# Retention and a feed-forward layer on one core: other orders of the same work in steps 0 to 31

## The chip, the core and the metric

The kernel runs on one core of one Trainium2 chip. Its engines work side by side, each through a queue of its own: TensorE (PE, matrix products), VectorE (DVE), ScalarE (ACT), GpSimd (POOL), and SyncE (SP), which here issues all transfers. The metric is the device time of one execution, in microseconds (us).

## What is computed

Eight batches of eight heads with 576 positions of 64 numbers go through a retention layer (scores with a decay by distance, no softmax); its result x, 4608 rows of 512, goes through a feed-forward layer whose activation is a quotient of two polynomials.

```python
scores = scale * np.matmul(q, k.transpose(0, 1, 3, 2))
Dmat = np.where(rel >= 0, gamma[:, None, None] ** rel[None, :, :], 0.0)
attn = np.matmul(scores * Dmat[None, :, :, :], v)
x = attn.transpose(0, 2, 1, 3).reshape(B * S, H * D)          # 4608 x 512
h = x @ w_in                                                  # 512 -> 2048
P = a[0] + a[1] * h + a[2] * h2 + a[3] * h3                   # h2 = h*h, h3 = h2*h
Q = 1.0 + np.abs(b[0]) * np.abs(h) + np.abs(b[1]) * h2
out = (P / (Q + 1e-06)) @ w_out                               # 2048 -> 512
```

## The kernel before

**Tiles.** The 4608 rows are 36 units of 128 rows; four units make a block of 512 rows (nine blocks). w_in and w_out are cut into 16 slices each. Every float32 operand of a big product is split into a high and a low part that TensorE takes in its fast float32 form, and three of the four products of parts are summed: xhi and xlo for x, w[:, 0] and w[:, 1] for a weight slice, g[:, 0] and g[:, 1] for the activation.

**Steps.** A step i handles one pair (block b, slice f). Steps 0 to 7 are block 0 with slices 0 to 7, steps 8 to 23 block 1 with all 16, steps 24 to 31 block 0 with slices 8 to 15; from step 32 on a block has 16 steps in a row. In the names of tiles the two numbers are block and slice (h0_7, p1_3), and a weight slice is w0_f (w_in) or w1_f (w_out).

**What a step consists of**, by function (lines 390 to 490):
- `gemm1` (12 matmuls) makes h of this step in one of two PSUM buffers `h`.
- `ffn_p`: ScalarE writes p and u = |h|, VectorE multiplies p by h. `ffn_p2`: VectorE, the last operation that reads h and so frees its buffer.
- `ffn_va` (ScalarE) and `ffn_v` (VectorE) make v, the denominator.
- One step later: `ffn_r` (ScalarE: Ln and Exp into u, the reciprocal), `ffn_q` and `ffn_q3` (VectorE: three operations on p, v and u).
- Two steps later: `ffn_hi` (ScalarE) and `ffn_lo` (GpSimd up to step 25, VectorE later) split p into the parts of g.
- `gemm2` (12 matmuls) three or four steps later adds g times w_out into two accumulators `acc`. When a block's last slice is done, ScalarE copies the accumulators to `o`; for block 0 this happens after slice 7 (step 11), and block 1 uses the same two buffers from step 12 on.

**Attention.** A *visit* (lines 297 to 311) finishes unit a and begins unit k on TensorE: at steps 0, 2, 4, 6, 23, 24, 26, 28, 30, then every fourth. The begun part lies in `y`, which takes one of the two `h` buffers, and in `ps`. Before it, `scale_q` (GpSimd, qk) and `scale_v` (ScalarE, eight small operations on kv) prepare unit k; after it, `decay`, `decay1` and `add` (VectorE) read y and ps, `fade` (GpSimd) scales the state S, and `keep_hi` (ScalarE) and `keep_lo` (VectorE) write xhi and xlo of unit a.

**Splitting weights.** During steps 0 to 23 the weights, loaded as raw bits, are split by `split_weight`: ScalarE makes two arrays (`start`), VectorE combines them in two operations on c (stages `split1` and `split2`), then ScalarE writes the high part w and GpSimd the low part w (`split3`). `split_step(j)` advances every split that has reached stage j, so a name that stands ahead of an earlier stage's name takes effect a step later.

**What sets the order.** Each engine runs its instructions in program order (class `InOrder`). Within a step the program order comes from a list of names, walked by `run`: `FIRST` in steps 0 to 7 and 21 to 23, `MID` in steps 8 to 20 (where u lies in PSUM, as `free_at`), `DENSE` in steps 24 to 31, `REST` later. A name whose work doesn't occur in a step is passed over.

Of the kernel before, what the change touches and what calls it, by code (L numbers as in the profile page):

```python
# [29 lines left out]
NF = DFF // P  # L30
# [1 line left out]

BEFORE = "split1 start scale_q scale_v visit_a decay visit_b add fade keep_hi keep_lo split2 split3 split0".split()
LAST_BEFORE = "visit_b keep_hi visit_a keep_lo start split1 decay add fade scale_q scale_v split2 split3 split0".split()
FIRST = (
    "split1 gemm1 visit ffn_p split2 ffn_p2 ffn_hi decay keep_hi ffn_lo gemm2 ffn_r scale_q split3 decay1 add fade keep_lo"
    " start scale_v split0 ffn_q ffn_q3 ffn_va ffn_v"
).split()
MID = (
    "split1 split2 gemm1 ffn_p ffn_r ffn_hi ffn_lo split3 ffn_va gemm2 ffn_p2 ffn_q ffn_v ffn_q3 start split0"  # L40
).split()
DENSE = (
    "gemm1 split1 ffn_p visit ffn_p2 decay keep_hi decay1 add fade keep_lo split2 split0 ffn_va ffn_v scale_q ffn_hi ffn_r"
    " ffn_lo scale_v gemm2 split3 ffn_q ffn_q3"
).split()
REST = (
    "gemm1 ffn_p visit ffn_p2 ffn_hi decay keep_hi ffn_lo decay1 add fade keep_lo scale_q scale_v ffn_va ffn_v gemm2 ffn_r"
    " ffn_q ffn_q3"
# [1 line left out]
END = "ffn_r ffn_hi gemm2 ffn_lo ffn_q ffn_q3".split()  # L50
# [5 lines left out]
VISITS = {0: (4, 5), 2: (5, 6), 4: (6, 7), 6: (7, None), 23: (None, 8)}  # L56
# [20 lines left out]
def retention_ffn(ctx: ExitStack, tc: tile.TileContext, qkv, w_in, w_out, ab, masks, gq, gv, out):  # L77
# [304 lines left out]
    free_at = []  # L382
# [110 lines left out]
    first = half + NF  # L493
# [4 lines left out]
    def lag(i):  # L498

        return 4 if NF // 2 <= i < first - 2 or i >= len(steps) - 8 else 3  # L500
# [6 lines left out]
    def load_weights(n):  # L507
        for k in [k for _, k in zip(range(n), loads)]:
            load_weight(k)
# [12 lines left out]
    def run(names, todo):  # L522
        todo |= {f"split{j}": (split_step, j) for j in range(4)}
        for name in names:
            if name in todo:
                todo[name][0](*todo[name][1:])
# [50 lines left out]
    for i in range(len(steps) + lag(len(steps))):  # L577
        this, prev, prev2 = (steps[j][:2] if 0 <= j < len(steps) else None for j in (i, i - 1, i - 2))
        todo = {"gemm2": (products, i), "start": (split_start, STARTS[i] if i < first else 0)}

        if i in VISITS:
            a, k = VISITS[i]
            todo["visit"] = visit, a, k
            if a is not None:
                todo |= {f.__name__: (f, a) for f in (keep_hi, keep_lo)}
            if k is not None:
                todo |= {f.__name__: (f, k) for f in ((decay, decay1, add, fade) if a is not None else (decay, add, fade))}
        if i + 1 in VISITS and VISITS[i + 1][1] is not None:
            todo |= {f.__name__: (f, VISITS[i + 1][1]) for f in (scale_q, scale_v)}
        if this:  # L590
            todo |= {f.__name__: (f, *this) for f in (gemm1, ffn_p, ffn_p2, ffn_va, ffn_v)}
        if prev:
            todo |= {f.__name__: (f, *prev) for f in (ffn_r, ffn_q, ffn_q3)}
        if prev2:
            todo |= {"ffn_hi": (ffn_hi, *prev2), "ffn_lo": (ffn_lo, *prev2, i - 2 < first)}
        if i == half:
            ps = ps_at.tile([P, 2, 512], F32, tag="at", name="free_at")
            free_at.extend((ps[:, 0], ps[:, 1]))
        elif i == FIRST_DENSE - 1:
            free_at.clear()  # L600
        run(END if not this else MID if free_at else FIRST if i < first else DENSE if i < 2 * NF else REST, todo)
        load_weights(2)


# [39 lines left out]
```

## Time and profile before

| | |
|---|---|
| median of 3 timed runs | 937.72 us (937.56 to 937.93) |
| the profiled execution, and its span from first to last instruction | 936.93 us, 935.1 us |
| busy share of the span: PE, DVE, ACT, POOL | 96%, 87%, 78%, 17% |
| mean granted TensorE clock | 0.985 |
| bytes moved by DMA | 65.50 MB |
| steps 0 to 12 in the trace | 33 to 132 us |

The profile comes from one execution. Its page and the trace name an instruction by line, engine, operation and tiles (`out<-in`); nearly all instructions have line 73, since they are issued through one helper, so the tiles tell them apart. "PE h waits for DVE p" means that TensorE, about to write into h, was last held back by VectorE's operation that writes p. In the order rows below, a name's last number is a buffer's own number, and L73 is L67 after the change, because the tables above it are shorter.

### The profile page before, as it was taken

The numbers are of one execution on the slowest core, as the hardware profiler recorded it, in microseconds if no ns is written. First come the engines' busy times: TensorE is split into PE (matmuls) and PEld (weight loads), VectorE is DVE, ScalarE is ACT, GpSimd is POOL, SyncE is SP. The second block draws the span as 40 slices with busy tenths as digits, with TensorE's granted clock in tenths as the row PEclk, the third lists the DMA queues.
The fourth block names the chain that finished last, engine by engine and source line by source line (L and its number), as shares of the span: only waits on it lengthen the run. The fifth ranks groups of instructions, "written<-read, shape, count | busy, mean of one in ns | idle before, by whom it ended". The sixth has DMA issues, their size and how long they took to land.

```text
span 935.1 us, 19368 instructions
## 1 busy us (share of the span) xinstructions
PE 898.5 (96%) x7852; PEld 735.5 (79%) x7852; DVE 814.1 (87%) x1219; ACT 727.8 (78%) x1306; POOL 155.3 (17%) x128
## 2 busy tenths in 40 slices
PE   7779889999999999999999999999999999999997
PEld 6667668877778888888888888888888888888886
DVE  2789989998988888888888898899888889888895
ACT  5778899988677778877787778777877787867775
POOL 3545444452100000000000000000000000000000
PEclk8789999999999999999999999999999999999999
DMA  9975000012221111211121112111211121001001
GB/s 335 374 296 178 5 0 1 1 46 91 91 71 66 47 46 46 81 43 36 39 81 43 47 46 91 46 46 47 90 47 47 46 91 46 1 2 45 1 1 45
DMA packets 20569, 65.50 MB, mean 70 GB/s; under 512 B 2432, under 2 KB 2432, under 8 KB 20480
## 3 DMA queue, kind: packets, MB, share of 16 engines
q1 hardware_dynamic: 20480, 64.28, 19.4%
q8 instruction: 61, 1.00, 0.5%
q14 instruction: 28, 0.23, 0.1%
HBM read 54.83 MB, written 9.44 MB: 69 GB/s over the span
## 4 chain that ended last, share of the span: by engine, by line
PE 46%; DVE 26%; ACT 22%; issue 3%; DMA 1%; SPq 0%; DVEq 0%; ACTq 0%
PE h L73 21%; PE acc L73 21%; DVE p L73 13%; DVE v L73 7%; ACT u L73 6%; ACT v L73 4%; ACT kv L73 4%; ACT g L73 3%; ACT free_at L73 2%; DVE c L73 2%; PE psNone L73 2%; PE ps L73 2%; DVE g L73 1%; DVE qk L73 1%; DVE xlo L73 1%
## 5 line engine op out<-in xcount | busy, mean ns | idle before, releaser
L73 PE MATMUL acc<-w,g 128*128 128x512 f32 x1632 | 398.7, 393 | 5.4 <-ACT o L73 4.1
L73 PE MATMUL h<-xhi,w 128*128 128x512 f32 x1152 | 383.4, 394 | 13.5 <-DVE p L73 13.5
L73 PEld LDWEIGHTS acc<-w,g 128*128 128x128 f32 x1632 | 304.4, 188 | 72.0 <-ACT o L73 4.5
L73 PEld LDWEIGHTS h<-xhi,w 128*128 128x128 f32 x1152 | 218.2, 189 | 66.7 <-DVE p L73 21.2
L73 PE MATMUL h<-xlo,w 128*128 128x512 f32 x576 | 225.9, 392 | 0.0
L73 ACT ACTIVATE p<-h,ab_sb 128x512 f32<-128x512 f32 x144 | 111.3, 773 | 72.2 <-PE h L73 64.2
L73 ACT ACTIVATE u<-h 128x512 f32<-128x512 f32 x131 | 78.2, 597 | 86.2 <-DVE v L73 85.8
L73 DVE SCALAR_TENSOR_TENSOR p<-p,ab_sb,u 128x512 f32<-128x512 f32 x131 | 120.9, 923 | 25.5 <-ACT u L73 20.2
L73 PEld LDWEIGHTS h<-xlo,w 128*128 128x128 f32 x576 | 109.1, 189 | 22.0
L73 DVE TENSOR_TENSOR v<-v,u 128x512 f32<-128x512 f32 x131 | 95.5, 729 | 30.0 <-ACT v L73 29.9
L73 DVE TENSOR_TENSOR p<-p,h 128x512 f32<-128x512 f32 x144 | 98.9, 687 | 17.2 <-ACT u L73 17.0
L73 DVE SCALAR_TENSOR_TENSOR p<-p,ab_sb,h 128x512 f32<-128x512 f32 x144 | 107.6, 747 | 4.7
L73 ACT ACTIVATE v<-u,absb 128x512 f32<-128x512 f32 x131 | 105.3, 804 | 0.5
L73 DVE SCALAR_TENSOR_TENSOR p<-v,p 128x512 f32<-128x512 f32 x144 | 99.6, 691 | 4.5
L73 POOL TENSOR_TENSOR S<-S,gv_sb 128x256 f32<-128x256 f32 x32 | 20.4, 636 | 484.1 <-DVE S L73 483.9
L73 ACT ACTIVATE u<-u,lnb 128x512 f32<-128x512 f32 x131 | 94.9, 724 | 4.3
L73 DVE SCALAR_TENSOR_TENSOR v<-v,u 128x512 f32<-128x512 f32 x131 | 97.1, 741 | 0.0
L73 ACT ACTIVATE u<-v,lnb 128x512 f32<-128x512 f32 x131 | 93.3, 712 | 0.9 <-DVE v L73 0.9
L73 ACT ACTIVATE g<-p 128x512 fp32r<-128x512 f32 x136 | 85.8, 631 | 10.0 <-DVE p L73 3.6
L73 DVE TENSOR_TENSOR g<-p,g 128x512 fp32r<-128x512 f32 x112 | 79.9, 714 | 1.4 <-ACT g L73 1.4
L73 ACT ACTIVATE kv<-kv,gv_sb 128x64 f32<-128x64 f32 x288 | 72.4, 335 | 8.5 <-DMA gv_sb<-in_gv 6.4
L73 POOL TENSOR_TENSOR qk<-qk,gq_sb 128x512 f32<-128x512 f32 x36 | 58.5, 1626 | 53.3 <-DMA qk<-in_qkv 53.2
(73 smaller groups left out, 731.7 us busy)
## 6 DMA issues: line engine op xcount, KB each, us to landing
qk<-in_qkv SPq DMA_DIRECT2D x36, 512.0 KB, 4.1
kv<-in_qkv SPq DMA_DIRECT2D x36, 512.0 KB, 5.8
bits<-in_w_in SPq DMA_DIRECT2D x16, 512.0 KB, 8.9
bits<-in_w_out SPq DMA_DIRECT2D x16, 512.0 KB, 7.5
out<-o SPq DMA_DIRECT2D x16, 512.0 KB, 3.3
out<-o SPq DMA_DIRECT2D x4, 256.0 KB, 2.3
gq_sb<-in_gq SPq DMA_DIRECT2D x1, 256.0 KB, 2.7
mask_sb<-in_masks SPq DMA_DIRECT2D x1, 32.0 KB, 6.0
```

The lines of the kernel that those rows point to most:

```text
L73: return lambda *a, **k: self.tc.keep_in_program_order(method(*a, **k))
```

## The change

The lists FIRST, MID and DENSE are replaced, and steps without a visit get lists of their own in place of FIRST and DENSE:

```diff
-FIRST = (
-    "split1 gemm1 visit ffn_p split2 ffn_p2 ffn_hi decay keep_hi ffn_lo gemm2 ffn_r scale_q split3 decay1 add fade keep_lo"
-    " start scale_v split0 ffn_q ffn_q3 ffn_va ffn_v"
-).split()
+FIRST = "split1 gemm1 visit ffn_p ffn_p2 ffn_hi split2 decay keep_hi ffn_lo gemm2 ffn_r scale_v scale_q split3 decay1 add fade start split0 keep_lo ffn_q ffn_q3 ffn_va ffn_v".split()
+FIRST_ALONE = "split1 split3 gemm1 visit gemm2 ffn_p split2 ffn_va ffn_p2 ffn_hi decay keep_hi ffn_lo ffn_r scale_q decay1 add keep_lo fade start scale_v split0 ffn_q ffn_q3 ffn_v".split()
...
+MID = "start split2 gemm1 ffn_p gemm2 ffn_r ffn_hi ffn_lo ffn_va split3 ffn_p2 ffn_q ffn_v ffn_q3 split0 split1".split()
-DENSE = (
-    "gemm1 split1 ffn_p visit ffn_p2 decay keep_hi decay1 add fade keep_lo split2 split0 ffn_va ffn_v scale_q ffn_hi ffn_r"
-    " ffn_lo scale_v gemm2 split3 ffn_q ffn_q3"
-).split()
+DENSE = "gemm1 ffn_p visit decay split0 ffn_p2 split1 scale_q ffn_hi ffn_r ffn_va ffn_lo scale_v gemm2 ffn_q split2 ffn_v keep_hi split3 ffn_q3 keep_lo decay1 add fade".split()
...
-        run(END if not this else MID if free_at else FIRST if i < first else DENSE if i < 2 * NF else REST, todo)
+        whole = i in VISITS
+        early = FIRST if whole else FIRST_ALONE
+        dense = DENSE if whole else DENSE_ALONE
+        run(END if not this else MID if free_at else early if i < first else dense if i < 2 * NF else REST, todo)
```

No instruction is added or taken away, and TensorE's products and visits follow one another as before. What moves on the other engines is shown at three places.

VectorE, step 0, which has a visit: p0_0 is the first step's p, c0_3, c1_0 and c0_4 are three weight splits, qk5 and kv5 belong to the visit. Before:

```order
L73 TENSOR_TENSOR p0_0_661<-p0_0_661,h0_0_582 128x512
L73 SCALAR_TENSOR_TENSOR c0_3_551<-bits0_3_276,c0_3_551 128x512
L73 SCALAR_TENSOR_TENSOR c1_0_554<-bits1_0_369,c1_0_554 128x512
L73 SCALAR_TENSOR_TENSOR c0_4_557<-bits0_4_371,c0_4_557 128x512
L73 SCALAR_TENSOR_TENSOR p0_0_661<-p0_0_661,ab_sb_98,h0_0_582 128x512
```

The same place after the change:

```order
L67 TENSOR_TENSOR p0_0_661<-p0_0_661,h0_0_582 128x512
L67 SCALAR_TENSOR_TENSOR p0_0_661<-p0_0_661,ab_sb_98,h0_0_582 128x512
L67 SCALAR_TENSOR_TENSOR c0_3_551<-bits0_3_276,c0_3_551 128x512
L67 SCALAR_TENSOR_TENSOR c1_0_554<-bits1_0_369,c1_0_554 128x512
L67 SCALAR_TENSOR_TENSOR c0_4_557<-bits0_4_371,c0_4_557 128x512
```

The operation with `ab_sb` and h (ffn_p2), the last reader of h0_0, has gone ahead of the three splits; the same holds in steps 2, 4, 6 and 23.

ScalarE, steps 5 and 6: g0_3, the Ln and Exp on u0_4, the high parts of w0_7 and w1_4, a new split (c1_5, bits1_5), v0_5, and p0_6 of the next step. Before:

```order
L73 ACTIVATE g0_3_1101<-p0_3_887 128x512
L73 ACTIVATE u0_4_1026<-v0_4_1027,lnb_111 128x512
L73 ACTIVATE u0_4_1026<-u0_4_1026,lnb_111 128x512
L73 ACTIVATE w0_7_1118<-c0_7_1062 128x512
L73 ACTIVATE w1_4_1121<-c1_4_1065 128x512
L73 ACTIVATE c1_5_1124<-bits1_5_743 128x512
L73 ACTIVATE bits1_5_743<-bits1_5_743 128x512
L73 ACTIVATE v0_5_1093<-u0_5_1092,absb_99 128x512
L73 ACTIVATE p0_6_1190<-h0_6_1137,ab_sb_98 128x512
```

After the change, from p0_6 on:

```order
L67 ACTIVATE p0_6_1184<-h0_6_1131,ab_sb_98 128x512
L67 ACTIVATE u0_6_1182<-h0_6_1131 128x512
L67 ACTIVATE g0_4_1189<-p0_4_1022 128x512
L67 ACTIVATE xhi1_671<-ps7_None_1144 128x4x128
L67 ACTIVATE u0_5_1104<-v0_5_1105,lnb_111 128x512
L67 ACTIVATE u0_5_1104<-u0_5_1104,lnb_111 128x512
L67 ACTIVATE w0_7_1208<-c0_7_1061 128x512
L67 ACTIVATE w1_4_1211<-c1_4_1064 128x512
L67 ACTIVATE w1_5_1214<-c1_5_1119 128x512
```

w0_7 and w1_4 have moved from step 5 to step 6, behind p0_6 and the Ln and Exp of step 5, and stand in a row with w1_5; GpSimd's low parts follow them. v0_5 has moved ahead of g0_3.

ScalarE, step 11, where block 0's accumulators are copied out (o0_0, o0_1; acc0). Before:

```order
L73 ACTIVATE p1_3_1448<-h1_3_1434,ab_sb_98 128x512
L73 ACTIVATE free_at_1284<-h1_3_1434 128x512
L73 ACTIVATE free_at_1284<-v1_2_1394,lnb_111 128x512
L73 ACTIVATE free_at_1284<-free_at_1284,lnb_111 128x512
L73 ACTIVATE g1_1_1454<-p1_1_1342 128x512
L73 ACTIVATE w0_10_1457<-c0_10_1425 128x512
L73 ACTIVATE v1_3_1447<-free_at_1284,absb_99 128x512
L73 ACTIVATE o0_0_7_1473<-acc0_0_0_897 128x1024
L73 ACTIVATE o0_1_7_1475<-acc0_0_1_898 128x1024
```

After:

```order
L67 ACTIVATE p1_3_1451<-h1_3_1437,ab_sb_98 128x512
L67 ACTIVATE free_at_1281<-h1_3_1437 128x512
L67 ACTIVATE o0_0_7_1467<-acc0_0_0_885 128x1024
L67 ACTIVATE o0_1_7_1469<-acc0_0_1_886 128x1024
L67 ACTIVATE free_at_1281<-v1_2_1397,lnb_111 128x512
L67 ACTIVATE free_at_1281<-free_at_1281,lnb_111 128x512
```

The two copies stand five rows earlier, right behind |h| of the step.

More of the change, by code (lines that the diff above doesn't have):

```diff
@@ L34 @@
 LAST_BEFORE = "visit_b keep_hi visit_a keep_lo start split1 decay add fade scale_q scale_v split2 split3 split0".split()
-FIRST = (
-    "split1 gemm1 visit ffn_p split2 ffn_p2 ffn_hi decay keep_hi ffn_lo gemm2 ffn_r scale_q split3 decay1 add fade keep_lo"
-    " start scale_v split0 ffn_q ffn_q3 ffn_va ffn_v"
-).split()
-MID = (
-    "split1 split2 gemm1 ffn_p ffn_r ffn_hi ffn_lo split3 ffn_va gemm2 ffn_p2 ffn_q ffn_v ffn_q3 start split0"
-).split()
-DENSE = (
-    "gemm1 split1 ffn_p visit ffn_p2 decay keep_hi decay1 add fade keep_lo split2 split0 ffn_va ffn_v scale_q ffn_hi ffn_r"
-    " ffn_lo scale_v gemm2 split3 ffn_q ffn_q3"
-).split()
+FIRST = "split1 gemm1 visit ffn_p ffn_p2 ffn_hi split2 decay keep_hi ffn_lo gemm2 ffn_r scale_v scale_q split3 decay1 add fade start split0 keep_lo ffn_q ffn_q3 ffn_va ffn_v".split()
+FIRST_ALONE = "split1 split3 gemm1 visit gemm2 ffn_p split2 ffn_va ffn_p2 ffn_hi decay keep_hi ffn_lo ffn_r scale_q decay1 add keep_lo fade start scale_v split0 ffn_q ffn_q3 ffn_v".split()
+MID = "start split2 gemm1 ffn_p gemm2 ffn_r ffn_hi ffn_lo ffn_va split3 ffn_p2 ffn_q ffn_v ffn_q3 split0 split1".split()
+DENSE = "gemm1 ffn_p visit decay split0 ffn_p2 split1 scale_q ffn_hi ffn_r ffn_va ffn_lo scale_v gemm2 ffn_q split2 ffn_v keep_hi split3 ffn_q3 keep_lo decay1 add fade".split()
+DENSE_ALONE = "gemm1 ffn_p visit decay keep_hi decay1 add ffn_r split1 fade keep_lo split2 ffn_p2 split0 ffn_va ffn_v scale_q ffn_hi ffn_lo gemm2 split3 scale_v ffn_q ffn_q3".split()
 REST = (
```

## The prediction

> **What bounds the kernel now.** First comes the table by stretches, cut where TensorE's behaviour changes. Its columns are the stretch, its length, busy time and instruction count of each engine, the granted TensorE clock, DMA share and GB/s.
>
> ```profile
> 33.00:131.77 98.77, 79.13 (x710) 62.22 (x707) 91.93 (x126) 84.42 (x154) 46.75 (x34) 0.93 0.45 162
> 131.77:190.00 58.23, 58.23 (x258) 48.21 (x257) 52.20 (x80) 54.94 (x92) 26.46 (x21) 1.00 0.00 1
> 190.00:280.00 90.00, 86.44 (x961) 69.55 (x960) 82.42 (x118) 68.57 (x139) 24.08 (x19) 1.00 0.22 76
> 280.00:900.00 620.00, 619.71 (x5220) 508.79 (x5219) 553.04 (x841) 481.16 (x840) 46.28 (x40) 1.00 0.14 48
> ```
>
> From 131.77 us to 190 TensorE never rests, and from 280 to 900 it rests 0.29 us: there only less matrix work would help, and the change leaves that work and its order alone. What an order can win lies in two places: 33 to 131.77 us (steps 0 to 12), where TensorE is idle for 98.77 - 79.13 = 19.64 us at a mean clock of 0.93, and 190 to 280, with 3.56 us idle. In the first, VectorE is busy 91.93 of 98.77 us (93%) and ScalarE 84.42 (85%), so these two set the pace. Second view: who TensorE waits for between 33 and 132 us (total, times, longest).
>
> ```profile
> PE h L73 <- DVE p L73: 13.4, 6, 4.3
> PE acc L73 <- ACT o L73: 4.1, 1, 4.1
> ```
>
> 17.5 of the 19.64 us are two waits. `h` waits for `p`: the products h have two PSUM buffers, and one is free again only when VectorE has done ffn_p2, the last operation that reads it. `acc` waits for `o`: ScalarE must have copied block 0's two accumulators out before block 1 may use them. Third view, TensorE in order of time (start, duration, idle time before and its releaser).
>
> ```profile
> 42.97 0.72 PE L73 MATMUL h<-xhi,w 128*128 128x512 f32 x1 [3.82 <-DVE p L73]
> ...
> 58.90 0.79 PE L73 MATMUL h<-xhi,w 128*128 128x512 f32 x1 [4.35 <-DVE p L73]
> ...
> 101.17 0.50 PE L73 MATMUL h<-xhi,w 128*128 128x512 f32 x1 [1.90 <-DVE p L73]
> ...
> 127.34 4.62 PE L73 MATMUL acc<-w,g 128*128 128x512 f32 x12 [4.08 <-ACT o L73]
> 131.77 0.43 PE L73 MATMUL h<-xhi,w 128*128 128x512 f32 x1
> ```
>
> A long gap costs twice: in the even stretch 258 matmuls take 58.23 us, so 12 take 2.71, but behind the gap of 4.08 us 12 take 131.77 - 127.34 = 4.43, 1.72 us more. Behind the gap of 1.90 us the first matmul takes a normal 0.50 us (0.72 and 0.79 behind the other two long ones).
>
> **The change, part by part.** No instruction is added or removed, and TensorE's blocks (h, attention, acc) keep their order; VectorE, ScalarE and GpSimd get the same rows in another order. So every term is a waiting time.
>
> *Term 1: in steps with a visit, ffn_p2 goes ahead of the weight splits.* VectorE at steps 0 and 2:
>
> ```profile
> 39.77 0.69 DVE L73 TENSOR_TENSOR p<-p,h 128x512 f32<-128x512 f32 x1 [0.90 <-ACT u L73]
> 40.37 1.89 DVE L73 SCALAR_TENSOR_TENSOR c<-bits,c 128x512 int32<-128x512 int32 x3
> 42.18 0.74 DVE L73 SCALAR_TENSOR_TENSOR p<-p,ab_sb,h 128x512 f32<-128x512 f32 x1
> ...
> 56.47 1.71 DVE L73 SCALAR_TENSOR_TENSOR c<-bits,c 128x512 int32<-128x512 int32 x1
> ```
>
> The row at 42.18 frees h0_0; TensorE starts h0_1 0.05 us after its end. With the three `c` behind it, it starts at 40.46, the end of the row at 39.77, and ends at 41.2: h0_1 starts near 41.27, 1.7 us earlier, behind a gap of 2.1 us. The three `c` end 0.7 us later, and ScalarE's three `w` and v0_0 with them, so ScalarE comes to p0_1 (47.62 below) at 45.4 at the earliest; h0_1 is done by then, at 44.0. In step 2 ffn_va of step 1 stands ahead of the scalings `kv`, and a `w` goes behind p0_2. ScalarE:
>
> ```profile
> 47.62 0.78 ACT L73 ACTIVATE p<-h,ab_sb 128x512 f32<-128x512 f32 x1 [2.77 <-PE h L73]
> ...
> 50.24 0.63 ACT L73 ACTIVATE w<-c 128x512 fp32r<-128x512 f32 x1
> ...
> 54.54 0.76 ACT L73 ACTIVATE p<-h,ab_sb 128x512 f32<-128x512 f32 x1
> ```
>
> From p0_1 to p0_2 are 6.9 us; without the `w` (0.63 us, 0.1 of it under the next row) 6.4: p0_2 starts at 51.8, and its u ends at 53.05. VectorE's ffn_p product (0.65) and ffn_p2 (0.74) follow at once, since the `c` of 1.71 us goes behind them: h0_3 starts near 54.55, **4.35 us earlier**.
>
> The gaps that stay, 2.0 to 2.7 us, lie between the rows of 1.90 us (no slow matmuls) and 3.82 us (slow). I take the nearer, no loss, and keep one loss of 1.72 us for the range. The Trainium skill, "TensorE: Matmul & The Clock Gate", section "HAM oscillation — how this bites in real kernels", warns only of idle gaps above some 3.4 us. By that rule all three slow starts vanish, and the sum stays as it is; if gaps of 2 us slowed it too, the sum would lose up to 1.72 us for each.
>
> *Term 2: steps 3 to 8.* Here VectorE does not rest (first row), and what counts is how long its operations take beside GpSimd:
>
> ```profile
> 65.53:101.17 35.64, 31.55 (x306) 25.03 (x304) 35.15 (x45) 30.27 (x55) 18.82 (x13) 1.00 0.37 124
> ...
> 61.42 0.68 DVE L73 SCALAR_TENSOR_TENSOR v<-v,u 128x512 f32<-128x512 f32 x1
> ...
> 71.18 1.75 DVE L73 SCALAR_TENSOR_TENSOR v<-v,u 128x512 f32<-128x512 f32 x1
> ...
> 68.97 3.41 POOL L73 TENSOR_TENSOR w<-c,w 128x512 fp32r<-128x512 f32 x2
> ```
>
> The same operation takes 0.68 us alone and 1.75 beside GpSimd's `w`: a meeting costs 1.07 us. Four small operations of 0.34 and 41 of 0.63 would take VectorE 27.2 us, so about 8 of its 35.15 are meetings: in order of time I count five whole and six half ones. Operations that read h, y or ps from PSUM keep their time. The Trainium skill, "GPSIMD Engine Reference", section "1. Specifications", states contention with GpSimd for every VectorE instruction with two SBUF inputs, which speaks against bunching `w`: by that rule alone all eight postponed `w` would cost a whole meeting, 8.6 us, and the sum would be 2.2 us smaller.
>
> In the new order ffn_p, ffn_p2 and the five operations of a visit follow one another, all from PSUM, beside GpSimd's `g` or `w`. Against that, steps 1, 3, 5 and 7 leave the last part of a split (ScalarE's `w`, GpSimd's `w`) to the next step, where two or three in a row meet the older product's three operations. Laid side by side, I find four whole and four half meetings: 8.6 - 6.4 = 2.2 us less, and the 0.5 us of idle time goes. But in step 3 two operations that ran clean now meet `w` (1.4 us of the 4.35 are lost). 4.35 - 1.4 + 2.7 = 5.6: h1_1, which waits for ffn_p2 of step 7, starts near 95.6 instead of 101.17, **5.6 us earlier**. Beside it lies a new wait, the late w0_7:
>
> ```profile
> 92.53 0.73 ACT L73 ACTIVATE u<-u,lnb 128x512 f32<-128x512 f32 x1
> ...
> 90.95 0.39 PE L73 MATMUL h<-xhi,w 128*128 128x512 f32 x1
> ```
>
> ScalarE now makes w0_7 behind that exponential (Exp of step 5), which itself comes some 6.8 us earlier, at 85.7; w0_7's high half is there at 86.3, GpSimd's low half at 87.6. TensorE, 6.9 us ahead, would start h0_7 at 84.0 (90.95 before) and waits 2.3 us, and 0.9 us more at its third matmul. It still reaches h1_1 at 95.4, just ahead of ffn_p2: cost nothing, but without cover beyond 0.2 us.
>
> *Term 3: the copies out of block 0* (step 11). ScalarE:
>
> ```profile
> 122.64 0.58 ACT L73 ACTIVATE free_at<-h 128x512 f32<-128x512 f32 x1 [0.23 <-DVE v L73]
> ...
> 126.27 1.94 ACT L73 ACTIVATE o<-acc 128x1024 f32<-128x1024 f32 x2
> ```
>
> The copies move from behind v1_3 to right behind |h| (the row of 122.64), from 126.27 to 123.2 if all else stood still. From h1_1 to acc of g1_0 TensorE has eight blocks of 12 matmuls, 2.71 us each, 21.7 us. I get a gap of 1.3 us before g1_0 and no other, since ffn_p2 of steps 8 to 10 comes 0.9 to 1.8 us before it is asked for: 23.0 us instead of 131.77 - 101.17 = 30.6, **7.6 us less**. ScalarE's Ln then stands 1.9 us behind the copies; ffn_p2 of step 12 is still done 0.4 us before h1_6 asks. Bound: 0 to 1.5 us; I take 0.
>
> *Term 4: steps 24 to 31.*
>
> ```profile
> 217.66 0.51 PE L73 MATMUL y<-kv 64*64 64x64 f32 x3 [0.75 <-ACT kv L73]
> ...
> 226.32 2.60 PE L73 MATMUL acc<-w,g 128*128 128x512 f32 x10 [0.29 <-DVE g L73]
> ```
>
> VectorE now finishes v1_15 earlier, which frees ScalarE's u0_9 and with it kv10, and `g` stands ahead of xlo: 0.75 + 0.29, and the latter again at the next visit, **1.3 us**. ffn_p2 now follows two copies of y (0.4 us each) and still ends over 1 us before the next h, because an acc block lies between.
>
> *SyncE's queue:* one weight load passes a load of q and k; both are needed tens of microseconds later. Nothing.
>
> *Sum:* 5.6 + 7.6 + 1.3 = 14.5 us. My walk leaves out hand-overs (0.05 us from VectorE to TensorE at 42.97); for some 30 new ones I take off 1.5: 13.0. The profiled execution took 936.93 us around its span of 935.1, the median of the timed runs 937.72. 937.72 - 13.0 = **924.7 us**.
>
> **The rivals.**
> 1. *VectorE keeps what term 1 wins.* Five more meetings eat 5.4 of the 5.6 us. Left: 0.2 + 7.6 + 1.3 - 1.5 = 7.6 us, 930.1. For it: the 93%; against: ffn_p2 alone passes 0.6 to 1.7 us of `c`, whatever VectorE's total is.
> 2. *Fewer meetings:* half of my 6.4 us go too, and hand-overs cost nothing: 13.0 + 3.2 + 1.5 = 17.7 us, 920.0.
> 3. *Slower: the late weights.* If the exponential stays at 92.53, w0_7's low half is there at 95.2, 3.8 us after h0_7's third matmul (two matmuls behind 90.95) wants it; with a slow clock 5.5. Each of eight bursts can cost one more meeting, 8.6 us. 14.1 us lost against 7.6 + 1.3: 5 us slower, 943. It decides once the bursts cost more than 8.9 us. Against: GpSimd gets no more work.
> 4. *The order doesn't matter,* since ScalarE (85%) is as late as VectorE: 937.7.
>
> **How the numbers follow.** Forecast 0.62, rival 1 0.20, rival 2 0.08, rivals 3 and 4 0.05 each. The range runs from rival 2 to rival 1 with one slow clock (1.72): 919.5 to 932. Faster by over 0.2% (1.9 us, about what a measurement of this kernel can tell from no change): 0.62 + 0.20 + 0.08 = 0.90; same 0.05; slower 0.05.
>
> **What would show it.** Term 1: h0_1 near 41.3, h0_3 near 54.6, gaps under 3 us, first matmuls of 0.5 us. Term 2: h0_7 waits 2 to 3 us for `w`; h1_1 near 95.6. Term 3: acc waits near 1.3 us for `o`, then 12 matmuls in 2.9 us; h1_5 near 118.6. Term 4: no wait of y for kv10. From 280 us on the same rows, moved by the sum. The prediction is wrong if VectorE takes as long for steps 3 to 7 as before, if h0_7 waits over 5 us, or if waits for `p` come up in steps 12 to 20.

## The result and the profile after

| | before | after |
|---|---|---|
| median of the timed executions (4 each) | 937.64 us | 922.91 us (921.64 to 923.27) |
| ratio to before, 95% interval | | 0.9842 (0.9825 to 0.9859) |
| profiled execution, its span | 936.93, 935.1 us | 922.57, 920.8 us |
| mean granted TensorE clock | 0.985 | 0.990 |
| h0_0 starts at | 33.32 us | 33.23 us |

One execution of MID alone below (3100.45 us, the one with the profile) and one of the kernel with kv earlier (1267.91 us) were in a slow state; the ratios leave them out.

The change saves 14.7 us; 924.7 us was forecast, with a range of 919.5 to 932. That the total came out so close is luck: two errors of some 3 us cancel, as the stretches show. The table by stretches of the changed kernel, cut at h1_5, at the visit of step 23 and at the first product of block 2 into the accumulators (columns as in the prediction):

```profile
33.00:121.94 88.94, 76.90 (x703) 60.71 (x700) 83.53 (x117) 79.85 (x148) 44.46 (x33) 0.93 0.50 180
121.94:183.97 62.03, 60.39 (x266) 49.23 (x264) 58.95 (x89) 60.45 (x104) 31.41 (x24) 1.00 0.00 1
183.97:263.68 79.71, 78.46 (x945) 64.47 (x945) 71.94 (x114) 64.35 (x133) 19.84 (x17) 1.00 0.24 81
263.68:886.00 622.32, 621.97 (x5229) 510.72 (x5230) 554.88 (x843) 481.54 (x841) 46.19 (x40) 1.00 0.14 49
```

The second and third stretch of the kernel before, cut at the same places:

```profile
131.77:192.19 60.42, 60.08 (x266) 49.40 (x264) 54.39 (x82) 56.50 (x95) 28.65 (x23) 1.00 0.00 1
192.19:278.13 85.94, 82.72 (x945) 66.78 (x945) 78.36 (x114) 66.68 (x137) 21.89 (x17) 1.00 0.22 75
```

The first stretch is 9.8 us shorter, the second 1.6 longer, the third 6.2 shorter. In the third TensorE does the same 945 matmuls in 78.46 us of busy time where it took 82.72: 4.3 us of "work" are gone, though no matmul was removed. That is the surprise of this case.

Who TensorE waits for in the changed kernel from 33 to 122 us (total, times, longest):

```profile
PE h L67 <- DVE p L67: 5.1, 4, 2.2
PE h L67 <- ACT w L67: 3.3, 1, 3.3
PE y L67 <- issue: 2.5, 2, 1.2
PE h L67 <- POOL w L67: 0.6, 1, 0.6
PE acc L67 <- ACT o L67: 0.4, 1, 0.4
```

The waits for `p` fell from 13.4 to 5.1 us and that for `o` from 4.1 to 0.4; one of 3.3 + 0.6 us for `w` is new. The two of 1.2 us put down to "issue" (no releaser in the trace) lie in the visits of steps 2 and 4; behind both visits the next h waits for `p` all the same (2.16 and 0.19 us). TensorE in order of time:

```profile
40.86 0.50 PE L67 MATMUL h<-xhi,w 128*128 128x512 f32 x1 [2.15 <-DVE p L67]
...
54.81 0.59 PE L67 MATMUL h<-xhi,w 128*128 128x512 f32 x1 [2.16 <-DVE p L67]
...
87.64 0.50 PE L67 MATMUL h<-xhi,w 128*128 128x512 f32 x1 [3.30 <-ACT w L67]
...
89.00 1.07 PE L67 MATMUL h<-xhi,w 128*128 128x512 f32 x2 [0.63 <-POOL w L67]
...
98.22 0.62 PE L67 MATMUL h<-xhi,w 128*128 128x512 f32 x2
...
119.06 3.04 PE L67 MATMUL acc<-w,g 128*128 128x512 f32 x12 [0.39 <-ACT o L67]
...
121.94 0.39 PE L67 MATMUL h<-xhi,w 128*128 128x512 f32 x1
```

These are h0_1, h0_3, h0_7 (two rows), h1_1 (the second matmul of the row at 98.22, so 98.45), g1_0 and h1_5. At 89.00 two matmuls take 1.07 us where two take 0.62 at 98.22: the clock had dropped.

### The profile page after: what moved, and what is told of

Its sections match the earlier page's. It is cut to its first block, busy times and chain, and to the rows that moved or that the text cites. A ratio compares the mean times of both kernels' runs of the same rounds, so it can differ in the third digit from the quotient of the medians.

```text
span 920.8 us, 19361 instructions
## 1 busy us (share of the span) xinstructions
PE 892.1 (97%) x7852; PEld 731.4 (79%) x7852; DVE 803.8 (87%) x1219; ACT 725.3 (79%) x1306; POOL 153.4 (17%) x128
## 4 chain that ended last, share of the span: by engine, by line
PE 50%; ACT 23%; DVE 20%; issue 4%; DMA 2%; POOL 0%; SPq 0%; DVEq 0%; ACTq 0%; POOLq 0%
PE h L67 23%; PE acc L67 23%; DVE p L67 11%; ACT u L67 6%; DVE v L67 5%; ACT v L67 4%; ACT kv L67 3%; ACT g L67 3%; ACT free_at L67 3%; PE ps L67 2%; PE psNone L67 1%; DVE c L67 1%; ACT p L67 1%; PE y L67 1%; ACT bits L67 1%
## 5 line engine op out<-in xcount | busy, mean ns | idle before, releaser
L67 DVE SCALAR_TENSOR_TENSOR p<-v,p 128x512 f32<-128x512 f32 x144 | 101.7, 706 | 4.4
L67 DVE SCALAR_TENSOR_TENSOR v<-v,u 128x512 f32<-128x512 f32 x131 | 94.3, 720 | 0.0
L67 ACT ACTIVATE g<-p 128x512 fp32r<-128x512 f32 x136 | 85.7, 630 | 9.7 <-DVE p L67 3.3
L67 DVE TENSOR_TENSOR g<-p,g 128x512 fp32r<-128x512 f32 x112 | 76.6, 684 | 1.4 <-ACT g L67 1.4
L67 POOL TENSOR_TENSOR qk<-qk,gq_sb 128x512 f32<-128x512 f32 x36 | 56.8, 1576 | 53.9 <-DMA qk<-in_qkv 53.9
```

What stands on the lines that cost most here:

```text
L67: return lambda *a, **k: self.tc.keep_in_program_order(method(*a, **k))
```

## The experiments

Since the start of h0_0 differs from execution to execution by up to 2 us (32.45 to 34.43), whatever the order, the table also has the time from there to the end of the span, in each kernel's profiled execution (for MID alone that of a second run, 933.13 us). Each ratio is to the kernel before on the same chip, whose median lay between 936.83 and 937.64 us, so it isn't the quotient of two rows of the table. The changed kernel's two profiles give 887.57 and 887.71 on this measure.

| kernel | median us | ratio to before (95%) | from h0_0 to the end, us |
|---|---|---|---|
| before | 937.64 | 1 | 901.78 |
| changed | 922.91 | 0.9842 (0.9825 to 0.9859) | 887.57 |
| changed, again | 923.75 | 0.9861 (0.9841 to 0.9882) | 887.71 |
| MID alone | 933.29 | 0.9961 (0.9947 to 0.9975) | 898.16 |
| DENSE lists alone | 933.16 | 0.9961 (0.9946 to 0.9975) | 897.11 |
| FIRST lists alone | 932.17 | 0.9949 (0.9934 to 0.9963) | 896.75 |
| changed, split3 early in steps 1, 3, 5, 7, 21, 22 | 925.08 | 0.9865 (0.9849 to 0.9882) | 889.27 |
| changed, split3 early in step 5 | 922.24 | 0.9836 (0.9820 to 0.9853) | 886.87 |
| changed, split3 early within step 6 | 921.31 | 0.9828 (0.9813 to 0.9844) | 886.61 |
| changed, gaps of steps 0 and 2 filled | 923.20 | 0.9848 (0.9834 to 0.9863) | 887.75 |
| changed, term 1 undone | 924.59 | 0.9872 (0.9855 to 0.9889) | 889.09 |
| before, kv earlier in DENSE | 938.96 | 1.0024 (1.0012 to 1.0036) | 903.71 |
| changed, w0_7, qk8 and kv8 earlier | 920.60 | 0.9827 (0.9810 to 0.9844) | 884.85 |

### One list at a time

Each of three kernels is the one before with one of the new lists (for FIRST and DENSE with its `_ALONE` partner):

```diff
-MID = ("split1 split2 gemm1 ffn_p ffn_r ffn_hi ffn_lo split3 ffn_va gemm2 ffn_p2 ffn_q ffn_v ffn_q3 start split0").split()
+MID = "start split2 gemm1 ffn_p gemm2 ffn_r ffn_hi ffn_lo ffn_va split3 ffn_p2 ffn_q ffn_v ffn_q3 split0 split1".split()
```

MID alone:

> Only the list MID is new; steps 0 to 7, 21 to 23 and 24 to 31 keep the old order. Theory (term 3 of the prediction, with the size that the changed kernel's trace has): TensorE's stretch from h1_1 to h1_5 falls from 30.6 to 23.4 us, and the visit of step 23 then waits up to 1.1 us longer, since the matmuls catch up with ScalarE and GpSimd: 930.4 to 931.5 us against 937.6. Rival (the copies' move needs the new early order to pay): h1_1 to h1_5 stays above 27 us, and the time above 934.

It took 933.29 us, 3.8 less: short of the theory, and not over 934 either. A second run was to tell where the rest goes:

> The kernel of the run with MID alone once more, for its trace. It gained 3.8 us where 6 to 7 were expected. Theory (the rest is lost ahead of the copies): h1_1 to h1_5 takes 26 to 27 us and not 23.4, because the waits of h for p in steps 9 and 10 (0.67 and 1.17 us before) stay or grow when VectorE has not been relieved in steps 0 to 7. Rival (lost later): h1_1 to h1_5 takes 23 to 24 us, and 2 to 3 us are lost in waits for qk and kv at steps 22 to 26.

The three stretches of TensorE in the profiled executions, from rows such as those above ("end" is the first product of block 2 into the accumulators, 278.13 us before, 263.68 after):

| | h0_0 to h1_1 | h1_1 to h1_5 | h1_5 to "end" |
|---|---|---|---|
| before | 67.85 | 30.60 | 146.36 |
| MID alone | 67.81 | 24.83 | 148.42 |
| DENSE lists alone | 67.67 | 30.61 | 141.95 |
| FIRST lists alone | 65.23 | 28.22 | 146.20 |
| changed | 65.22 | 23.49 | 141.74 |

MID alone gives 5.8 us up to h1_5; with 24.83 us this stretch lies between theory and rival. 2.1 us go later, as the rival said, but only about half of them in the waits that it named. TensorE, at g1_0 and at the visit of step 23, and the block of acc behind that visit (the granted clock is the third number from the end):

```profile
123.01 3.04 PE L73 MATMUL acc<-w,g 128*128 128x512 f32 x12 [0.37 <-ACT o L73]
...
187.84 0.69 PE L73 MATMUL psNone<-qk 64*64 64x64 f32 x32 [1.34 <-POOL qk L73]
...
190.81 5.49 PE L73 MATMUL acc<-w,g 128*128 128x512 f32 x12
```

```profile
190.81:196.10 5.29, 5.29 (x14) 4.13 (x14) 5.00 (x7) 4.63 (x9) 3.24 (x3) 0.50 0.00 0
```

The gap before g1_0 is 0.37 us instead of 4.08 and its 12 matmuls run at full clock; then the visit waits 1.34 us for qk8 where it had waited 0.34. The next block of acc takes 5.49 us, 3.02 before, and waits for nothing: the granted clock is 0.50 there. The visit of step 24 behind it, 1.7 us shorter than before, takes most of that back. In the changed kernel the same visit waits 1.42 us for qk8 and the clock stays up behind it, so this loss may belong to the execution and not to the list.

The DENSE lists alone:

> Only DENSE and DENSE_ALONE are new (steps 24 to 31). Theory (the visits' matmuls wait for kv one head at a time, which the trace counts as busy; of the three long visits only that of step 26 has its kv from a step with these lists): the visit of step 26 falls from 4.2 to about 1.8 us, three waits for g go (1.9 us), those of steps 23 and 24 stay long: 3.3 to 4.3 us less, 933.3 to 934.3 us. Rival (term 4 of the prediction, as large as the waits that the trace lists): 1.3 us less, 936.3.

4.0 us less, as the theory had it, and three times what the prediction's term 4 gave. What the long visit is made of shows in the kernel before: TensorE's first row of the visit of step 26 and the block of acc behind it, then a block of acc that waits for g, and the h after it.

```profile
215.66 0.69 PE L73 MATMUL ps<-qk,kv 64*64 64x64 f32 x32
...
219.83 3.03 PE L73 MATMUL acc<-w,g 128*128 128x512 f32 x12
...
225.42 0.61 PE L73 MATMUL acc<-w,g 128*128 128x512 f32 x2
...
228.76 0.39 PE L73 MATMUL h<-xhi,w 128*128 128x512 f32 x1
```

The same places with the DENSE lists alone:

```profile
216.14 0.67 PE L72 MATMUL ps<-qk,kv 64*64 64x64 f32 x29
...
217.93 0.50 PE L72 MATMUL acc<-w,g 128*128 128x512 f32 x1
...
223.51 2.88 PE L72 MATMUL acc<-w,g 128*128 128x512 f32 x12
...
226.23 0.39 PE L72 MATMUL h<-xhi,w 128*128 128x512 f32 x1
```

The visit takes 217.93 - 216.14 = 1.79 us instead of 219.83 - 215.66 = 4.17, though the trace lists one wait of 0.75 us in it. ScalarE, before:

```profile
217.27 2.00 ACT L73 ACTIVATE kv<-kv,gv_sb 128x64 f32<-128x64 f32 x8
```

It scales kv10 head by head in 2.00 us from 217.27 on, while the matmuls of the visit follow it: each waits a little, and these waits are counted as busy time. The block of acc takes 226.23 - 223.51 = 2.72 us instead of 228.76 - 225.42 = 3.34, a loss of 0.62 where 0.29 is listed, and there were three of these, 1.8 us together. 2.38 + 1.8 = 4.2 us, against 146.36 - 141.95 = 4.4 measured.

The FIRST lists alone:

> Only FIRST and FIRST_ALONE are new (steps 0 to 7 and 21 to 23). Theory: h1_1 starts near 98.5 us as in the changed kernel (2.7 us earlier than before), the gap before g1_0 stays at about 4 us, and the visits of steps 23 and 24 fall from 2.8 and 3.75 to 1.6 and 2.0 us, because kv9 is scaled ahead of the weights of step 23: 5.7 us less in all, less up to 1 us for qk8: 932 to 933 us. Rival (the order of steps 21 to 23 is without effect, all the late gain comes from DENSE): 2.7 us less, 935.

The time fits the theory (932.17), but its places don't all: h1_1 comes 2.6 us earlier, and another 2.4 are won between h1_1 and h1_5, since VectorE is no longer behind there. Before g1_0 the old gap stands. The visits of steps 23 and 24 do fall from 2.8 and 3.75 to 1.5 and 2.0 us, but h1_5 to "end" gains only 0.16: the next h waits 1.42 us for VectorE instead, and the visit of step 26 takes 4.6 us. Nor is the fall at step 24 due to these lists alone: MID alone, with the old FIRST, has 2.02 us there, and the second profile of the changed kernel 3.70 (the last section says what goes with it).

```profile
122.68 4.43 PE L72 MATMUL acc<-w,g 128*128 128x512 f32 x12 [3.90 <-ACT o L72]
...
201.27 0.50 PE L72 MATMUL h<-xhi,w 128*128 128x512 f32 x1 [1.42 <-DVE p L72]
```

From h0_0 on the three lists alone give 3.6, 4.7 and 5.0 us, 13.3 together; all at once give 14.2.

### The late w0_7

The changed kernel with `split3` of FIRST_ALONE where FIRST has it:

```diff
-FIRST_ALONE = "split1 split3 gemm1 visit gemm2 ffn_p split2 ffn_va ffn_p2 ffn_hi decay keep_hi ffn_lo ffn_r scale_q decay1 ..."
+FIRST_ALONE = "split1 gemm1 visit gemm2 ffn_p split2 ffn_va ffn_p2 ffn_hi decay keep_hi ffn_lo ffn_r scale_q split3 decay1 ..."
```

> The changed kernel with split3 of FIRST_ALONE moved back behind scale_q, so w0_7 and w1_4 are made in step 5 and not in step 6. Theory (the late w0_7 is what holds TensorE from 84 to 98 us): h0_7 has no wait for w (3.3 and 0.6 us in the changed kernel), no slow clock behind it, and h1_1 starts near 95.6 us where VectorE sets it: 2.8 us less than the changed kernel, 920.1. Rival 1 (VectorE is as late anyway, the wait costs nothing): 922.9 and h1_1 still near 98.5. Rival 2 (the weights in step 5 meet VectorE's operations again): h1_1 later than 99.5 and 924 or more.

925.08 us is what rival 2 said, but not by its mechanism. The interval overlaps the changed kernel's; in the profiles it is 1.7 us slower from h0_0 on. TensorE in the visit of step 2, at h0_3 and at h1_1:

```profile
52.51 0.51 PE L67 MATMUL y<-kv 64*64 64x64 f32 x3 [0.62 <-ACT kv L67]
...
56.83 0.79 PE L67 MATMUL h<-xhi,w 128*128 128x512 f32 x1 [1.74 <-DVE p L67]
...
99.47 0.50 PE L67 MATMUL h<-xhi,w 128*128 128x512 f32 x1 [2.70 <-DVE p L67]
```

h0_7 has no wait now; but with the last `w` back in steps 1 and 3, ScalarE scales kv later and the visits of steps 2 and 4 stretch, and h0_5 starts 41.76 us behind h0_0, not 38.25. All of it is won back by h1_1, which comes 99.47 - 34.13 = 65.34 us behind h0_0, as in the changed kernel (65.22); the 1.7 us go later. Several places were moved at once, so a second kernel moves `split3` in step 5 alone (a list FIRST_5, used for `i == 5`), where ScalarE otherwise waits for VectorE:

> The changed kernel with split3 behind scale_q in step 5 alone; w0_7 and w1_4 are then made in step 5, where ScalarE otherwise waits 1.5 us for VectorE's v. Theory (the late w0_7 holds TensorE; the run with split3 moved in all steps without a visit lost the same in steps 1 to 4): h0_7 starts near 84.3 us without a wait, h1_1 near 94.4 to 96 us: 2.5 to 4 us less than the changed kernel, 919 to 920.4. Rival (VectorE is as late without this wait): h1_1 after 97.5, 922 to 923.

and a third keeps it in step 6, but earlier within the step (a list FIRST_6, used for `i == 6`):

```diff
+FIRST_6 = "split1 gemm1 visit ffn_p split3 ffn_p2 ffn_hi split2 ...".split()
```

> The changed kernel with w0_7 and w1_4 made in step 6 as before, but right behind p0_6 and u0_6 and ahead of g, xhi, Ln and Exp. Theory: w0_7 comes about 2.4 us earlier, h0_7 waits 0.9 us and not 3.3, the clock behind it stays up, and h1_1 starts near 95.5 us: 2 to 3 us less than the changed kernel, 920 to 921. Rival (the delay of g, xhi, Ln and Exp by 1.1 us costs as much): 922.5 to 924.

Step 5 alone: h0_7 starts without a wait, then TensorE waits 0.94 us for g and 3.29 for p.

```profile
85.21 0.39 PE L68 MATMUL h<-xhi,w 128*128 128x512 f32 x1
...
89.75 2.56 PE L68 MATMUL acc<-w,g 128*128 128x512 f32 x10 [0.94 <-POOL g L68]
...
98.32 0.50 PE L68 MATMUL h<-xhi,w 128*128 128x512 f32 x1 [3.29 <-DVE p L68]
```

Early within step 6, TensorE:

```profile
86.15 0.50 PE L68 MATMUL h<-xhi,w 128*128 128x512 f32 x1 [0.73 <-ACT w L68]
...
88.00 0.73 PE L68 MATMUL h<-xhi,w 128*128 128x512 f32 x2 [1.12 <-POOL w L68]
...
98.00 0.50 PE L68 MATMUL h<-xhi,w 128*128 128x512 f32 x1 [1.75 <-DVE p L68]
```

From h0_0 to h1_1 it is 98.32 - 34.43 = 63.89 and 98.00 - 34.29 = 63.71 us, where the changed kernel has 65.22. So the late w0_7 costs 1.3 to 1.5 us there: more than nothing, less than the 2.5 to 4 that I then expected, because VectorE comes next (waits of 3.29 and 1.75 us for `p`). VectorE is later there, too: between ffn_p2 of step 2 and of step 7 its operations that take over 0.8 us lose 9.2 and 9.3 us beyond 0.68 us each, 8.4 in the changed kernel, so the meetings with GpSimd that rival 2 named are part of it. At the end 0.7 and 1.0 us are left; in the second kernel a slow clock behind the visit of step 23 (185.53 to 188.95 us) takes some. The medians alone don't tell these two from the changed kernel, and that of step 5 alone is its rival's.

### TensorE's clock

The changed kernel with idle matmuls in the gaps behind the visits of steps 0 and 2:

```diff
+        if i == 0:
+            filler.append(ps_acc.tile([P, 2, 512], F32, tag="acc", name="filler"))
+        if i in (0, 2):
+            for _ in range(FILL):
+                pe.matmul(filler[0][:, 0, 0:P], gq_sb[:, 0], gq_sb[:, 0], start=True, stop=True)
```

> The changed kernel with 14 more matmuls (128x128, into accumulators that nothing reads) behind the visits of steps 0 and 2, about 1.7 us of work in gaps of 2.15 us. Theory (a slow clock behind these gaps costs nothing, since ScalarE comes to p0_1 and p0_3 only when TensorE is done): the slow matmuls of h0_1 and h0_3 go, h1_1 stays near 98.5 us, and the time is the changed kernel's, 922.4 to 922.9 us. Rival 1 (each slow clock costs its 1.7 us whole, as the low end of the prediction's range had it): 3.4 us less, 919.5. Rival 2 (the clock depends on more than this gap): the matmuls stay slow although the gap is filled.

```profile
37.90 2.16 PE L68 MATMUL filler<-gq_sb 128*128 128x128 f32 x17
...
41.58 0.48 PE L68 MATMUL h<-xhi,w 128*128 128x512 f32 x1
...
70.57 0.50 PE L68 MATMUL h<-xhi,w 128*128 128x512 f32 x1 [0.19 <-DVE p L68]
```

These are the filler of step 0 (17 of the 28 records that its 14 matmuls leave), h0_1 and h0_5. The filler ran longer than the gap and delayed h0_1, which starts 41.58 - 32.45 = 9.13 us behind h0_0 and not 40.86 - 33.23 = 7.63. In return the clock stays up (h0_1 and h0_2 end 14.85 us behind h0_0, 14.97 in the changed kernel), and h0_5 starts 38.12 us behind h0_0, where it was 38.25. At step 2 the filler delays h0_3 by 0.8 us, its block still ends 0.8 us earlier, and h0_5 gains next to nothing from it either. The time is the changed kernel's. The slow clock in these two places costs nothing, as the theory said: VectorE, busy 34.76 of the 35 us from 59 to 94 in the changed kernel, sets h0_5. (The prediction's range has one slow clock at its slow end, and none at its fast end.)

### Term 1 alone, and kv alone

```diff
-FIRST = "split1 gemm1 visit ffn_p ffn_p2 ffn_hi split2 decay ..."
+FIRST = "split1 gemm1 visit ffn_p split2 ffn_p2 ffn_hi decay ..."
```

> The changed kernel with split2 ahead of ffn_p2 again in the steps with a visit (term 1 undone, all else new). Theory (VectorE runs without a rest from p0_3 to h1_1, so what term 1 wins at p0_3 is kept to h1_1): h0_1 and h0_3 come 1.5 to 4 us later, h1_1 starts at 100.5 to 101.5 us instead of 98.5, and the time is 2 to 3 us above the changed kernel, 925 to 926. Rival (rival 1 of the prediction: VectorE keeps what term 1 wins): h1_1 stays within 0.7 us of 98.5, and the time of 922.9.

```profile
42.52 0.79 PE L67 MATMUL h<-xhi,w 128*128 128x512 f32 x1 [3.49 <-DVE p L67]
...
57.82 0.80 PE L67 MATMUL h<-xhi,w 128*128 128x512 f32 x1 [3.64 <-DVE p L67]
...
90.01 0.80 PE L67 MATMUL h<-xhi,w 128*128 128x512 f32 x1 [2.63 <-ACT w L67]
```

h0_1 and h0_3 come 1.7 and 3.0 us later, h1_1 1.7 (66.94 us behind h0_0, not 65.22), the end 1.5. So more than half of term 1's gain reaches h1_1; the rest, 1.3 us, stands against the waits for w0_7, which shrink from 3.30 and 0.63 to 2.63 and 0.14 us. The time, 924.59, is a little below the theory's, and its interval overlaps the changed kernel's: here the trace decides.

The last one changes only the kernel before: `scale_v` right behind `ffn_p` in DENSE.

```diff
-    "gemm1 split1 ffn_p visit ffn_p2 ... scale_q ffn_hi ffn_r"
-    " ffn_lo scale_v gemm2 split3 ffn_q ffn_q3"
+    "gemm1 split1 ffn_p scale_v visit ffn_p2 ... scale_q ffn_hi ffn_r"
+    " ffn_lo gemm2 split3 ffn_q ffn_q3"
```

> The kernel before with one name moved: scale_v stands right behind ffn_p in DENSE, so in step 25 ScalarE scales kv10 ahead of v, g, Ln and Exp. Theory (the matmuls of the visit of step 26 wait for kv one head at a time, and the trace counts these waits as busy): that visit falls from 4.2 to about 1.9 us, 2.4 us less at its end, of which the later v, g and Ln may cost some: 934.8 to 936. Rival (the wait costs what the trace lists, 0.75 us): the visit stays above 3.3 us.

```profile
215.56 0.64 PE L73 MATMUL ps<-qk,kv 64*64 64x64 f32 x28
...
217.35 0.74 PE L73 MATMUL acc<-w,g 128*128 128x512 f32 x2
218.70 2.57 PE L73 MATMUL acc<-w,g 128*128 128x512 f32 x10 [0.61 <-POOL g L73]
222.37 0.50 PE L73 MATMUL h<-xhi,w 128*128 128x512 f32 x1 [1.10 <-DVE p L73]
```

The visit falls to 217.35 - 215.56 = 1.79 us: the wait is kv, and it is worth 2.4 us. But v, g and Ln then come 2 us later on ScalarE, and the waits for g and p behind this visit and for g behind the next two take more than was won: 0.24% slower than before. The time that was expected was too low.

### Two waits of the changed kernel taken away

The list FIRST_6 from above and, in step 22, `scale_q` first and `scale_v` ahead of `start`:

```diff
+FIRST_22 = "scale_q split1 split3 gemm1 visit gemm2 ffn_p split2 ffn_va ffn_p2 ffn_hi decay keep_hi ffn_lo ffn_r scale_v ... start split0 ...".split()
-        early = FIRST if whole else FIRST_ALONE
+        early = FIRST_6 if i == 6 else FIRST_22 if i == 22 else FIRST if whole else FIRST_ALONE
```

> The changed kernel with w0_7 and w1_4 made early in step 6 (as in the run before that changed only this) and, in step 22, scale_q first and scale_v ahead of the start of a split. Theory: the first is worth 1.1 us at h1_5; the second takes away the wait of 1.4 us for qk8 at the visit of step 23 but for 0.1 to 0.4 us: 2.1 to 2.4 us less than the changed kernel, 920.5 to 920.8. Rival (a wait ahead of a later visit takes the place of the one for qk8): 921.5 to 922.

Beside it ran the changed kernel again:

> The changed kernel itself once more, beside the other three: 922.9 us. Its second trace shows which rows differ from run to run: the grid of the slow stretches of TensorE's clock may fall otherwise, the waits for w0_7 (3.3 us), o (0.4) and qk8 (1.4) should stand again.

920.60 us (919.21 to 921.26) against 923.75 (922.34 to 924.28) in executions on the same chip, and 2.7 us less from h0_0 on, as the theory had it: this version beats both kernels. The visit of step 23 has no wait for qk8:

```profile
180.32 0.69 PE L69 MATMUL psNone<-qk 64*64 64x64 f32 x32
...
193.80 0.47 PE L69 MATMUL h<-xhi,w 128*128 128x512 f32 x1 [0.83 <-DVE kv L69]
```

The wait of 0.83 us for VectorE's copy of y, 0.77 in the changed kernel, is the next one in line. The second profile of the changed kernel has its waits for w0_7 (3.30), o (0.38) and qk8 (1.41) again. Its h0_1 ran at full clock, behind a gap of 1.07 us, and h0_5 still starts 37.97 us behind h0_0, next to the 38.25 of the first.

## Why the prediction was right, and where its steps were not

Counted from h0_0, the span fell by 14.2 us: 2.6 up to h1_1, 7.1 from there to h1_5, 4.6 from there to "end", and nothing behind it (656.97 and 657.12 us). Against that stand the prediction's 5.6, 7.6 and 1.3, less 1.5 for hand-overs.

- **Term 1** held as put: h0_1 at 40.86 (41.27 forecast), h0_3 at 54.81 (54.55). The clock dropped behind both gaps, which I had not taken; the filled gaps show that this cost nothing.
- **Term 2** gave 2.6 us and not 5.6. VectorE did most of its part: ffn_p2 of step 7, the row below, ends at 96.55 where it ended at 101.11, 4.6 us earlier. The meetings came out nearly as walked: between ffn_p2 of step 2 and of step 7 VectorE's operations that take over 0.8 us lose 8.4 us beyond 0.68 us each, 9.0 before, so 0.6 less where the walk has 2.2 - 1.4 = 0.8.

```profile
95.81 0.74 DVE L67 SCALAR_TENSOR_TENSOR p<-p,ab_sb,h 128x512 f32<-128x512 f32 x1
```

  The step that failed is "It still reaches h1_1 at 95.4, just ahead of ffn_p2: cost nothing". TensorE waited 3.3 us for w0_7 and not 2.3. Most of that is a slip: the walk has the exponential start at 85.7 and w0_7 there at 86.3, though the exponential takes 0.73 us and a `w` 0.63 more, which makes it 87.1 (87.6 measured). The clock, down behind the gap of 3.30 + 0.63 us, took the rest: h1_1 started at 98.45, 1.9 us after its buffer was free. Here a slow clock did lie on the path. With w0_7 earlier, h1_1 gains 1.3 to 1.5 us, and VectorE ends the wait.
- **Term 3** held: 23.49 us from h1_1 to h1_5 (23.0 forecast), the gap before g1_0 0.39 us (1.3), full clock behind it. MID alone gives 5.8 us there. That the catch-up would be asked for again, 1.1 us more of waiting for qk8 at step 23, was not in the sum. And h1_6 waits 0.22 us for `p`, where the walk had 0.4 us in hand: small, but one of the prediction's own signs of being wrong.
- **Term 4** was mis-sized: "1.3 us" was a sum of listed waits, with two of the three for g. The mechanism was right (the wait for kv10 goes, and those for g), but the visit was worth 2.38 us, and each of three waits for g some 0.6. The DENSE lists alone bring 4.4. The visits of steps 23 and 24, 1.3 and 1.7 us shorter in the first profile, add hardly more (4.4 against 4.6): the waits for qk8 and for VectorE's copies of y take it back. In the second profile that of step 24 takes 3.70 us again.
- **Hand-overs:** 1.5 us were taken off for them. No run shows this loss; the walk from row to row did not need it.
- **Rivals.** Rival 1 (VectorE keeps term 1's gain) fell with the run that undoes term 1: 1.7 of 3.0 us reach h1_1. Rival 2 (half of the meetings go) didn't come, with 8.4 us of them left of 9.0, and rival 4 fell with the result. Rival 3's mechanism, the late weights, was there, at 1.3 to 1.5 us and not 5.5, and without more meetings of VectorE and GpSimd.

## What to carry to other kernels

Price a wait by the distance from block start to block start, in the place with the wait and in one without, not by the idle time listed: matmuls that wait one by one for small pieces count as busy, and 0.75 us listed were 2.4. When an order makes one engine earlier, look for the operand that another engine now makes last, count from the end of the operation ahead of it, and add the clock if the gap is long. And check a sum term by term against the stretches even when the total fits: here one term was 3 us too large and another 3.3 too small.

## What the runs showed of the hardware that was not expected

TensorE's slow clock comes in stretches of 3.4 us or a multiple of it (in the kernel before the granted clock is 0.50 from 56.8 to 63.5 us, around the end of the gap of 4.35), and the length of the gap ahead alone doesn't set it. In the changed kernel, behind the gaps of 2.15, 2.16 and 3.30 us (the granted clock is the third number from the end):

```profile
41.30:44.80 3.50, 3.50 (x10) 2.74 (x9) 3.23 (x8) 3.30 (x6) 2.60 (x2) 0.52 0.94 281
55.00:58.40 3.40, 3.40 (x9) 2.62 (x9) 3.40 (x7) 3.40 (x7) 2.31 (x3) 0.51 0.96 355
88.90:92.30 3.40, 3.30 (x8) 2.63 (x9) 3.37 (x3) 1.56 (x3) 3.40 (x3) 0.54 0.01 2
```

With split3 early in step 5, at the same h0_1 (TensorE's row, then the stretch behind it):

```profile
42.48 0.50 PE L68 MATMUL h<-xhi,w 128*128 128x512 f32 x1 [2.13 <-DVE p L68]
```

```profile
42.50:46.00 3.50, 3.50 (x15) 2.90 (x16) 3.50 (x8) 2.88 (x6) 2.17 (x2) 1.00 0.93 290
```

2.13 us left the clock up where 2.15 took it down, and in the run with split3 early in all steps without a visit 2.70 us ahead of h1_1 did not take it down (0.50 us for the first matmul). The slow matmul of that run behind 1.74 us (h0_3, 0.79 us) says nothing on the gap: the granted clock is 0.50 from 53.40 us on, during the visit, before the gap begins at 55.09. In each profile the stretches start and end on a grid of 3.413 us; in the changed kernel they start at 41.42, 55.07 and 89.20 us, 4 and 10 periods apart. The Trainium skill, "TensorE: Matmul & The Clock Gate", section "What's actually happening", has activity watched in a free-running window of 3413 ns; the stretches and the grid agree with that, and so does a gap that counts or not by where it falls. Its rule of thumb in "HAM oscillation — how this bites in real kernels", no gaps above some 3.4 us, would let the gaps of 2.15 and 2.16 us pass, and here the clock fell behind both.

In the visit of step 24 a wait with no releaser that the trace shows ("issue") comes and goes between executions of the same program: none in the first profile of the changed kernel, 1.36 us in the second. In the 13 profiles at hand it goes with a transfer of 16 KB on the DMA queue that the page calls "instruction" (q8). In seven such a transfer starts 0.4 to 1.3 us behind the visit's first matmul, and TensorE stops and goes on 1.2 to 1.6 us after the transfer's end; in the other six none starts within the visit, and there is no wait. That TensorE waits for its instructions there is likely, but no run moved the transfers to show it.
